# Loading q in 1024-byte rows, four tokens to a partition, with a new order for the first third of a fused retention and token-mixing kernel

## The chip, the cores and the metric

The kernel runs on one core of one Trainium2 chip. The metric is device time in microseconds (us) of one execution. The kernel before has a median of 165.22 us over three runs (165.19 to 165.68).

The engines are named as in the profile: PE is the matrix engine (TensorE) and PEld its weight loads, DVE is VectorE, ACT is ScalarE, POOL is GpSimd, and SP is the sync engine, which only issues transfers. ACT and POOL can issue transfers too, between their other instructions. A row that ends in q, such as SPq or ACTq, is such an issue.

## The reference

There are 4 batches, 8 heads, 768 tokens and a head width of 64, all in float32. Stage one is a recurrent linear attention (RetNet) with a decay per head. Stage two mixes the tokens of its output.

```
state = gamma * state + outer(k_t, v_t)        # per batch and head, t = 0..767
x_t   = q_t @ state / sqrt(64)                 # x: (4, 768, 512), heads side by side
theta = x @ w_theta
y     = w_tok_r @ (x * cos(theta)) + w_tok_i @ (x * sin(theta))     # over tokens
u     = x + y
out   = u + max(u @ w_ch, 0)
```

## The kernel before

**Tiles.** Stage one works in 24 units. Unit n covers one batch, 256 tokens and four heads: a batch has three groups of 256 tokens, and each group has two halves of the heads. For each unit there are three loads of 256 KB (`Lk`, `Lq`, `Lv`, all by `load_unit`, L157). Partition p of a loaded tile holds the tokens 2p and 2p+1 of each of the four heads, so a contiguous row of DRAM is 2 x 64 x 4 = 512 bytes, and a load has 512 such rows.

**Steps of a unit.** The names are those of the order below; the last letter of a token gives the engine or queue (p POOL, v DVE, a ACT, s SP).

- `ck`, `cq` cast k and q to bf16. `cqs` is `cq` with a decay factor (`qsc`) multiplied in, for units whose output is not scaled later by `XA`, and `cv` multiplies v by its factor (`vsc`).
- `Tk`, `Tq` transpose them on PE (L316), and `E` moves the result to SBUF (`kqT`). For some later units a DMA transpose (`Dk`) does both.
- `A` is the score matmul (L346), 16 pieces; `m` multiplies by the causal mask on DVE (L355, 1.2 us).
- `Y` applies the masked scores to v (L423), `I` adds the part from the state (L411), `ST` makes the state's update (L373).
- `S0`, `S1` add up the state, `SB` casts it to bf16 blocks, `XB` or `XA` takes the output out of PSUM into `xT` (`XA` with the decay factor `qx`).

**Steps of stage two**, for each chunk of 128 tokens: `Tx`, `Ex` (or the DMA `Dx`) transpose x; `Hh` is theta (L469, four matmuls 512 wide); `CN` takes sine and cosine on ACT; `z` makes both products; `M.t.s` are the two token-mixing matmuls of output tile t and input chunk s (L509); then `u`, `Tu`/`Eu` or `Du`, `O` (L536), `f`, and the store `SO`. `Tw`, `Ew` transpose the token weights, which `Pw` loads on POOL's own queue, like `Pth` and `Pch` for the other two weights. `Z` is a pair of matmuls on zeros whose result nobody reads.

**The order is written out by hand.** The string `ORDER` lists every step; each engine executes its own steps in that order and waits where data is missing. Nothing is rescheduled. Buffers: 16 for k and q together, 9 for v, 4 for `kqT`, two PSUM banks for transposes, one for scores.

**Transfers.** The framework gives the transfers of SP's and ACT's queues one of eight semaphores in turn, in the order of the string. A transfer is issued only after the transfer eight places before it has landed. So the eight places bound how far loads run ahead, and a queue (or the engine that owns it) stands still until then.

**Start.** `const1` to `const9` and `constA` make the constants: `const2` (POOL memsets and an iota, then a DVE product `arg`), `const3` (ACT: the factors `qsc` and `vsc`), `const8` and `const9` (ACT: eight exponentials for `qx`, L233), `const5` the mask, `const4` the identity, `const6` zeros in the state blocks.

Of the kernel before, what the change touches and what calls it, by code (L numbers as in the profile page):

```python
# [33 lines left out]
SB.5.0.v Tx.3 Tw.1.0 z.1.v SB.5.1.a Ew.1.0.v Ex.3.a CN.2.1 A.6 I.5 Y.5 ST.6 XA.5.0 z.2.v Tw.0.0  # L34
CN.3.0 Tx.4 CN.3.1 Ew.0.0.v S0.6.v XA.5.1 Ex.4.v Hh.4 CN.4.0 CN.4.1 Tw.0.1 M.0.1 Pw.1.1 z.3.v M.0.0
Tw.0.2 Pw.1.2 Ew.0.2.a SB.6.1.a Hh.5 z.4.p SB.6.0.p Lk.9.a M.0.3 ck.7.p cqs.7.p M.0.2 CN.5.1 CN.5.0
cq.8.v m.6 Ew.0.1.v Tw.1.1 Tw.1.2 Ew.1.1.v Lv.9.s M.0.4 M.1.0 Tx.5 Ew.1.2.v M.1.1 S1.6 Tk.7 M.1.4
Pch Ex.5.v z.5.v cv.7.v Tq.8 Tq.7 M.1.2 E.7.a M.0.5 I.6 Y.6 ST.7 A.7 ck.8.a u.0 S0.7.v m.7 XA.6.1
SB.7.1.a M.1.5 M.1.3 XA.6.0 Tw.1.3 M.2.5 Pw.0.2 M.2.3 u.1 S1.7 Tk.8 M.2.1 M.2.0 SB.7.0.v Ew.1.3.a
Tu.0 I.7 cv.8.v E.8.a Lk.10.s ck.10.p cv.9.p Y.7 ST.8 A.8 cqs.9.v ck.9.v M.2.4 Du.1 Eu.0.a XB.7.1.a  # L40
XB.7.0.v S0.8.v SB.8.0.v M.2.2 Tx.6 Tq.9 Tk.9 Lv.10.a cv.10.p Lq.10.s S1.8 u.2 m.8 O.0 E.9.a
SB.8.1.a Hh.6 Tw.1.4 I.8 Y.8 A.9 CN.6.0 Du.2 Lq.14.s CN.6.1 Ex.6.v f.0 ST.9 Tw.0.3 Hh.7 Ew.1.4.v
Ew.0.3.a S0.9.v Tw.0.4 M.3.0 Tw.1.5 CN.7.0 CN.7.1 M.3.2 Dx.7 M.3.1 M.3.5 M.3.3 Lv.12.s Lk.12.s
Ew.1.5.v XA.8.1 Ew.0.4.v Lq.12.s M.3.4 u.3 S1.9 Tw.0.5 Tk.10 M.4.5 cqs.10.p XA.8.0 m.9 M.4.3 Tq.10
SB.9.1.a SB.9.0.a I.9 O.2 Lq.11.s Lk.11.s E.10.a Lk.15.s Ew.0.5.v Lk.14.s Y.9 ST.10 A.10 z.7.p
# [54 lines left out]
def kernel(  # L100
# [13 lines left out]
    nc = tc.nc  # L114
# [532 lines left out]
```

## Time and profile before

| what | value |
|---|---|
| median of the runs | 165.22 us |
| span of the profiled execution, first to last instruction | 163.6 us |
| PE busy | 155.2 us (95%) |
| DVE, ACT, POOL busy | 114.0, 78.9, 74.3 us |
| bytes moved | 34.93 MB, mean 214 GB/s |
| the three kinds of loads | 256 KB each, 5.2 to 6.6 us from issue to landing (median by kind and queue) |
| granted PE clock | 1.000 |

The span leaves out what lies before the first and after the last instruction: 165.22 - 163.6 = 1.6 us against the median of the runs. For the profiled execution itself the span is the only time given. Starts in the answers of the trace are counted from the first instruction. In the page's second part each digit is the busy share of a slice of 4.1 us, and the digits for DMA give the mean over sixteen DMA engines. A row of the windows gives the DMA share as a fraction that can be above 1, since packets of one engine overlap.

### The profile page before, as it was taken

What the parts mean: (1) busy time and instruction counts of PE and PEld (TensorE: products, weight loads), DVE (VectorE), ACT (ScalarE), POOL (GpSimd) and SP (SyncE); (2) the same over time, 40 slices, a digit from 0 to 9 for tenths busy, and PEclk for the clock granted to TensorE, in tenths of its full rate; (3) what the DMA queues carried; (4) which work ended last, traced back from release to release, by engine and by line L of the source; (5) the groups of instructions that cost most, each with busy time, mean ns of one, the idle gap of its engine ahead of it and who ended that gap; (6) DMA issues with size and microseconds to landing.
All of it is one profiled execution on the core that took longest, in us unless ns stands there. A gap on an engine that the chain in (4) does not pass through costs nothing.

```text
span 163.6 us, 4928 instructions
## 1 busy us (share of the span) xinstructions
PE 155.2 (95%) x2034; PEld 87.2 (53%) x2034; DVE 114.0 (70%) x215; ACT 78.9 (48%) x140; POOL 74.3 (45%) x107
## 2 busy tenths in 40 slices
PE   5996889999999999999999999999999999999992
PEld 1453655656666655654554565554545554444561
DVE  3388687887994895984879894887867760345372
ACT  4976697974658255773343726732341616000020
POOL 7557389075034552730227599950469204600000
PEclk9999999999999999999999999999999999999999
DMA  3999999999999999999999999999897548515546
GB/s 115 297 290 255 268 283 236 275 220 286 220 162 232 223 291 139 338 203 270 324 263 198 134 268 221 242 193 298 125 245 136 103 92 227 160 64 128 129 164 224
DMA packets 69062, 34.93 MB, mean 214 GB/s; under 512 B 26416, under 2 KB 66096, under 8 KB 69040
## 3 DMA queue, kind: packets, MB, share of 16 engines
q1 hardware_dynamic: 56032, 23.73, 69.4%
q10 hardware_dynamic: 10320, 7.47, 17.7%
q0 software_dynamic: 2688, 3.41, 12.1%
q8 instruction: 16, 0.26, 0.7%
q14 instruction: 6, 0.05, 0.1%
HBM read 25.69 MB, written 6.29 MB: 196 GB/s over the span
## 4 chain that ended last, share of the span: by engine, by line
PE 76%; DMA 8%; ACT 5%; POOL 3%; issue 2%; SPq 2%; DVE 1%; POOLq 0%; ACTq 0%
PE y_ps L509 36%; PE o_ps L536 11%; PE th_ps L469 10%; DMA kqf<-in_k_dram 8%; PE r_ps L423 3%; ACT qx L233 3%; PE w_ps L491 3%; PE at_ps L346 3%; PE r_ps L411 2%; PE kq_ps L316 2%; SPq L157 2%; PE y_ps L561 2%; ACT cs L476 1%; PE x_ps L455 1%; PE r_ps L373 1%
## 5 line engine op out<-in xcount | busy, mean ns | idle before, releaser
L509 PE MATMUL y_ps<-z,wtr 128*128 128x512 bf16 x138 | 52.4, 380 | 0.0
L509 PE MATMUL y_ps<-z,wti 128*128 128x512 bf16 x138 | 52.3, 379 | 0.0
L483 POOL TENSOR_TENSOR z<-cs,x_sb 128x1024 bf16<-128x1024 bf16 x12 | 25.5, 2136 | 17.9 <-ACT cs L476 10.0
L355 DVE TENSOR_TENSOR at<-at_ps,mask 128x1024 bf16<-128x1024 f32 x24 | 29.2, 1216 | 0.2
L469 PE MATMUL th_ps<-wth,xT 128*128 128x512 bf16 x96 | 24.5, 379 | 0.5 <-ACT cs L476 0.4
L516 DVE TENSOR_TENSOR u<-y_ps,x_sb 128x512 bf16<-128x512 f32 x23 | 15.8, 688 | 12.7 <-PE y_ps L509 12.6
L542 DVE SCALAR_TENSOR_TENSOR ot<-o_ps,u 128x512 f32<-128x512 f32 x22 | 15.1, 688 | 12.5 <-PE o_ps L536 12.4
L308 POOL TENSOR_TENSOR vb<-vf,vsc 128x512 bf16<-128x512 f32 x15 | 15.6, 1041 | 17.3 <-DMA vf<-in_v_dram 16.9
L476 ACT ACTIVATE cs<-th_ps,zerob 128x512 bf16<-128x512 f32 x24 | 16.4, 685 | 13.3 <-PE th_ps L469 8.8
L536 PE MATMUL o_ps<-wch,uT 128*128 128x512 bf16 x88 | 22.6, 379 | 0.0
L476 ACT ACTIVATE cs<-th_ps,halfpi 128x512 bf16<-128x512 f32 x24 | 16.3, 686 | 11.5 <-issue 5.4
L509 PEld LDWEIGHTS <-wtr 128*128 128x128 bf16 x138 | 13.5, 98 | 12.7
L509 PEld LDWEIGHTS <-wti 128*128 128x128 bf16 x138 | 13.5, 98 | 12.0 <-issue 0.2
L139 POOL CAST sbd<-s 64x256 bf16<-64x256 f32 (+1 forms) x21 | 10.1, 481 | 20.8 <-DVE s L391 17.7
L137 ACT COPY kqT<-kq_ps 128x1024 bf16<-128x1024 bf16 x12 | 12.1, 1012 | 11.9 <-PE kq_ps L316 11.9
L469 PEld LDWEIGHTS <-xT 128*128 128x128 bf16 x96 | 8.8, 98 | 8.7 <-issue 0.5
L137 ACT CAST kqb<-kqf 128x512 bf16<-128x512 f32 x16 | 9.6, 620 | 6.9 <-DMA kqf<-in_k_dram 6.3
L536 PEld LDWEIGHTS <-uT 128*128 128x128 bf16 x88 | 8.1, 98 | 8.3
L278 PE MATMUL zz<-zero 128*128 128x512 bf16 x30 | 10.3, 476 | 1.9 <-DVE zero L192 1.9
L423 PE MATMUL r_ps<-at,vb 64*64 64x128 bf16 x384 | 9.9, 221 | 1.6 <-DVE at L355 1.6
L316 PE MATMUL kq_ps<-ident,kqb 128*128 128x128 bf16 x120 | 11.2, 220 | 0.3 <-POOL kqb L302 0.3
L139 POOL CAST kqb<-kqf 128x512 bf16<-128x512 f32 x12 | 7.2, 612 | 8.5 <-DMA kqf<-in_k_dram 8.4
(80 smaller groups left out, 208.7 us busy)
## 6 DMA issues: line engine op xcount, KB each, us to landing
vf<-in_v_dram SPq DMA_DIRECT2D x20, 256.0 KB, 5.9
kqf<-in_k_dram SPq DMA_DIRECT2D x19, 256.0 KB, 5.3
kqf<-in_q_dram SPq DMA_DIRECT2D x17, 256.0 KB, 5.8
out_dram<-ot ACTq DMA_DIRECT2D x12, 256.0 KB, 2.7
out_dram<-ot SPq DMA_DIRECT2D x11, 256.0 KB, 2.9
kqf<-in_q_dram ACTq DMA_DIRECT2D x7, 256.0 KB, 5.2
kqf<-in_k_dram ACTq DMA_DIRECT2D x5, 256.0 KB, 6.6
vf<-in_v_dram ACTq DMA_DIRECT2D x4, 256.0 KB, 5.8
```

Source lines behind the costliest of these rows:

```text
L137: nc.scalar.copy(dst, src)
L139: engines[e].tensor_copy(dst, src)
L308: engines[e].tensor_mul(in_blocks(vb), by_token(raw["vf", n]), _bcast_last(K["vsc"][:, i, :, h * HU:(h + 1) * HU], D))
L355: nc.vector.tensor_mul(at.rearrange("p g j a t -> p (g j) (a t)"), st["at_ps", n].rearrange("p g j a t -> p (g j) (a t)"), _bcast_mid(K["m ...
L423: nc.tensor.matmul(st["R", n + 1][c][g * D:(g + 1) * D, j * P:(j + 1) * P], st["vb", n][rows, lo:lo + D], st["at", n][rows, g, j, a, :], s ...
L469: nc.tensor.matmul(th_ps, st["xT", C][:, j, :], K["wth"][:, j, :], start=(j == 0), stop=(j == 3))
L476: nc.scalar.activation(st["cs", C][:, w, :], st["th_ps", C], AF.Sin, bias=K["zerob" if w else "halfpi"], scale=1.0)
L483: engines[e].tensor_mul(st["z", b][:, c], st["cs", C], _bcast_mid(x_of(C), 2))
L509: nc.tensor.matmul(st["y", t], K["wT"][r][:, s0, t0 * P:(t0 + 1) * P], st["z", b][:, s0, r, :], start=(done == 0 and r == 0), stop=(done = ...
L516: nc.vector.tensor_add(st["u", t], st["y", t], st["x", b][:, t0, :])
L536: nc.tensor.matmul(o_ps, st["uT", t][:, j, :], K["wch"][:, j, :], start=(j == 0), stop=(j == nD - 1))
L542: nc.vector.scalar_tensor_tensor(st["ot", t], st["o", t], 0.0, st["u", t], ALU.max, ALU.add)
```

## The change

Four things are changed.

1. **q's layout and its load.** `Lq` no longer uses `load_unit`. A unit's q is loaded by two transfers of 128 KB, one for each pair of heads. Each fills 64 partitions: partition p of a half holds the four tokens 4p to 4p+3 of two heads, so a row of DRAM is 1024 bytes. The bytes are the same. SP and ACT issue 158 transfers instead of 134, since each of the 24 units now takes two places for q in the round of eight semaphores.
2. **What follows from the layout.** The factor `qsc` gets its own argument `argq`: `const2` has two more iotas and eight more memsets of 64 partitions on POOL, and one more product on DVE. The mask, the casts, the transposed q (`qT`), and the write to `xT` use four-token patterns in place of two-token ones. Sizes of all instructions on PE, DVE, ACT and POOL stay the same: the score and state matmuls read their 128 moving columns in four runs of 32 instead of two of 64.
3. **The order of the first third**, some 420 steps up to `u.3 S1.9 Tw.0.5 Tk.10`, is new on all engines, transfers included. From there on the string is the same as before.
4. Among the steps that change engine in that third: `ck.0` POOL to ACT, `ck.1` ACT to DVE, `ck.2` ACT to POOL, `ck.3` POOL to ACT; `cv.0`, `cv.3` DVE to POOL; `cqs.0`, `cqs.2` DVE to POOL, `cqs.1` POOL to DVE; `E.3`, `E.4` ACT to DVE; `S0.0` DVE to ACT; `XB.1.0`, `XB.1.1`, `XB.3.0`, `XB.3.1` DVE to ACT; `z.3`, `cv.7` and `cqs.9` DVE to POOL; the issues of `Lk.1`, `Lk.3`, `Lv.7`, `Lv.8`, `Lv.9`, `Lq.8`, `Lq.9`, `Lk.10`, `Lq.14` SP to ACT, and that of `Lq.1` ACT to SP.

```
 ORDER, the old first third up to unit 6:
-const2 Lv.0.s const1 const6.v Z.29 Z.2 const5 Z.38 Lk.0.a const3 Z.35 Z.8 Lq.0.s Lv.1.s Z.28 constA
-const4 Lq.1.a const9 Lk.1.s Z.39 const8 ck.0.p Tk.0 ck.1.a cqs.0.v cv.0.v Tq.0 E.0.v Lq.4.a ST.0
-Lk.4.a cqs.1.p Tq.1 Lq.2.s S0.0.v SB.0.1.v A.0 Lk.2.s SB.0.0.p cv.1.p Lv.2.s S1.0 Z.15 I.0 Z.27 m.0
-Tk.1 E.1.a cqs.2.v Z.34 cv.2.p Y.0 ST.1 XB.0.1.a S0.1.v S1.1 SB.1.0.a Pth Lq.3.s Z.18 XB.0.0.v Tq.2
-A.1 SB.1.1.a ck.2.a I.1 m.1 Y.1 ST.2 Tk.2 const7 Z.23 XB.1.0.v Lk.3.s E.2.v XB.1.1.v A.2 ck.3.p
-S0.2.v m.2 S1.2 SB.2.1.a Z.11 cqs.3.p Tq.3 Lv.3.s Tx.0 Tk.3 Z.3 ck.4.p Lv.4.s Lk.5.s Lq.5.s Lv.5.s
-Lq.6.s Lk.6.s Lv.6.s Lq.7.s E.3.a SB.2.0.v I.2 Y.2 XB.2.1.a Ex.0.a cv.3.v cq.4.p Tk.4 Lq.8.s A.3
-ST.3 Lk.7.s S0.3.v SB.3.0.a S1.3 Lv.7.s Lk.8.s Tx.1 Tq.4 SB.3.1.p cv.4.p m.3 Pw.1.0 XB.2.0.a Ex.1.a
-I.3 Lv.8.s E.4.a ck.5.a cq.5.a Y.3 Pw.0.0 ST.4 Hh.0 S0.4.v XB.3.0.v XB.3.1.v cv.5.v CN.0.1 A.4
-CN.0.0 Tq.5 Hh.1 Tk.5 SB.4.0.p SB.4.1.a Pw.0.1 Hh.2 m.4 E.5.v I.4 Y.4 ST.5 ck.6.a Tk.6 Tx.2 cq.6.a
-CN.1.1 CN.1.0 XA.4.1 A.5 XA.4.0 m.5 Lq.9.s Ex.2.v S0.5.v z.0.p Tq.6 E.6.a CN.2.0 cv.6.p Hh.3
 the new one:
+Lv.0.s Lq.0.s const2 Lk.0.a const1 const6.v Z.29 Z.2 const5 Lk.1.a Z.38 const3 constA const4 const9 Z.35
+ck.0.a Z.8 Lq.1.s ck.1.v cv.0.p cqs.0.p Lv.1.s Z.28 Z.39 ST.0 Z.27 Lq.4.a Lq.2.s cqs.1.v Tk.0 cv.1.p Pth
+S0.0.a Tq.0 Tk.1 S1.0 E.0.v Tq.1 Z.23 Lk.3.a Lk.4.a Lk.2.s A.0 Z.11 m.0 SB.0.0.p SB.0.1.a ck.2.p Lv.2.s
+E.1.a const8 I.0 Y.0 ST.1 A.1 cqs.2.p Lq.3.s S0.1.v SB.1.1.p XB.0.0.v m.1 cv.2.p S1.1 Lv.3.s Tq.2 Z.18
+Z.15 Lv.5.s cqs.3.p Z.34 XB.0.1.a SB.1.0.a Tk.2 E.2.v I.1 Y.1 Lv.4.s ck.3.a ST.2 S0.2.v A.2 XB.1.1.a
+Tk.3 XB.1.0.a SB.2.1.p S1.2 Tx.1 cv.3.p Tq.3 m.2 SB.2.0.a Z.3 cq.4.p ck.4.p Ex.1.a I.2 Y.2 E.3.v Lk.5.s
+ST.3 A.3 S0.3.v const7 Tx.0 Hh.0 SB.3.0.a cv.4.p m.3 Ex.0.a Lq.5.s SB.3.1.v Lv.6.s XB.2.0.a XB.2.1.a
+Lq.6.s Hh.1 S1.3 CN.0.1 cv.5.v Pw.1.0 Tk.4 CN.1.1 Pw.0.0 Tq.4 E.4.v CN.1.0 I.3 Lk.6.s Y.3 ST.4 S0.4.v
+XB.3.0.a Pw.0.1 A.4 cq.5.v SB.4.1.a SB.4.0.p Lq.7.s XB.3.1.a Tq.5 ck.5.a Hh.2 Tk.5 m.4 Pw.1.1 Tx.2 I.4
+CN.0.0 cv.6.p Y.4 z.1.v E.5.v ST.5 A.5 cq.6.a S0.5.v ck.6.a Tk.6 Ex.2.v XA.4.1 Lk.7.s Tq.6 Hh.3 CN.2.1
+XA.4.0 SB.5.1.p SB.5.0.a z.0.p m.5 E.6.a Tw.1.0 I.5 CN.2.0 Tx.3 Ew.1.0.v Y.5 ST.6 Ex.3.a A.6 CN.3.0
...
     def Lq(n, e):
-        load_unit("qf", q, n, e)
+        b, i, h = unit(n)
+        t = io.tile([P, 2, 4, D], FT, name="kqf", bufs=16)
+        for j in range(2):
+            h0 = h * HU + 2 * j
+            queues[e].dma_start(
+                out=t[j * D:(j + 1) * D].rearrange("p g a d -> p g (a d)"),
+                in_=q[b, h0:h0 + 2, i * 2 * P:(i + 1) * 2 * P, :].rearrange(
+                    "g (p a) d -> p g (a d)", a=4))
+        raw["qf", n] = t
...
+        posq = const.tile([P, nI, 4], FT, name="posq")
+        lgq = const.tile([P, H // 2], FT, name="lgq")
+        for j in range(2):
+            rows = slice(j * D, (j + 1) * D)
+            nc.gpsimd.iota(posq[rows], pattern=[[2 * P, nI], [1, 4]], base=1,
+                           channel_multiplier=4, allow_small_or_imprecise_dtypes=True)
+            for x in range(H // 2):
+                head = x // 2 * HU + 2 * j + x % 2
+                nc.gpsimd.memset(lgq[rows, x:x + 1], math.log(gammas[head]))
...
+        argq = const.tile([P, nI * 4, H // 2], FT, name="argq")
+        nc.vector.tensor_mul(argq, _bcast_last(posq.rearrange("p i a -> p (i a)"), H // 2),
+                             _bcast_mid(lgq, nI * 4))
+        K["argq"] = argq
...
+    def qT(n, rows, j, c):
+        lo = j * D + c * (D // 2)
+        return st["kqT", n][rows, 1, :, lo:lo + D // 2]
...
                         nc.tensor.matmul(at_ps[cols, g, j, a, :],
-                                         kqT[rows, 0, a, j, cols],
-                                         kqT[rows, 1, :, j, cols],
+                                         kqT[rows, 0, 2 * a + j, cols],
+                                         qT(n, rows, j, c),
...
                 nc.tensor.matmul(r[c][:, j * P:(j + 1) * P], sbd_of(n)[:, c, j, :],
-                                 st["kqT", n][:, 1, :, j, c * D:(c + 1) * D],
+                                 qT(n, slice(0, P), j, c),
...
-        return (st["xT", C][:, 2 * h:2 * h + 2].rearrange("p j (t a) -> p j t a", a=2),
-                st["R", n + 1][c][:, :2 * P].rearrange("p (j a t) -> p j t a", j=2, a=2))
+        return (st["xT", C][:, 2 * h:2 * h + 2].rearrange("p j (t a) -> p j t a", a=4),
+                st["R", n + 1][c][:, :2 * P].rearrange("p (j a t) -> p j t a", j=2, a=4))
```

More of the change, by code (lines that the diff above doesn't have):

```diff
@@ new lines @@
+XB.10.1.a CN.8.0 SB.11.1.p cv.12.p Lq.16.s I.11 Tk.14 Ex.8.v A.12 Y.11 ST.12 f.4 Lv.15.s O.3 z.8.p
+E.14.a XA.11.0 XA.11.1 Hh.10 S0.12.a f.3 SB.12.0.v Tx.10 Tu.5 CN.10.1 Dx.11 Ex.10.v cq.13.p Lk.16.s
+Lv.17.s Hh.11 SO.2.s CN.10.0 m.12 S1.12 z.10.v Tk.15 M.6.1 M.6.2 M.6.0 M.6.3 CN.11.0 CN.11.1 M.7.3
+SB.12.1.a Lk.17.a ck.13.a M.7.4 M.7.0 M.6.4 Dk.13 M.7.1 z.11.v M.6.5 SO.3.s A.14 M.7.2 Eu.5.v I.12
+Lv.14.s u.6 cqs.15.v M.7.5 M.9.3 Tq.15 ck.17.a E.15.a m.14 SO.4.a Lq.17.s Lq.18.s Lk.21.s ck.16.a M.9.0
@@ L236, in const3 @@
     def const3():
-        K["qsc"] = const.tile([P, nI, 2, H], FT, name="qsc")
+        K["qsc"] = const.tile([P, nI, 4, H // 2], FT, name="qsc")
         K["vsc"] = const.tile([P, nI, 2, H], FT, name="vsc")
-        for t, bias, sc in ((K["qsc"], K["lscale"], 1.0), (K["vsc"], K["zerob"], -1.0)):
-            nc.scalar.activation(t.rearrange("p i a h -> p (i a) h"), K["arg"], AF.Exp,
+        for t, arg, bias, sc in ((K["qsc"], K["argq"], K["lscale"], 1.0),
+                                 (K["vsc"], K["arg"], K["zerob"], -1.0)):
+            nc.scalar.activation(t.rearrange("p i a h -> p (i a) h"), arg, AF.Exp,
                                  bias=bias, scale=sc)
@@ L259, in const5 @@
     def const5():
-        mask = const.tile([P, 2, 2, D], BF, name="mask")
+        mask = const.tile([P, 2, 4, D // 2], BF, name="mask")
         nc.gpsimd.memset(mask, 1.0)
```

113 lines of the change are left out of this document (53 added, 60 removed).

## The prediction

> **What bounds the kernel now.** I read the page's slices first, then PE's waits, then the chain that ended last, and then the places in time of the score matmuls.
>
> ```profile
> span 163.6 us, 4928 instructions
> ...
> PE   5996889999999999999999999999999999999992
> ...
> DMA  3999999999999999999999999999897548515546
> ```
>
> PE is full from the eighth slice (28.6 us) to the last. Only the first seven slices have room, and there the transfers are full too. The kernel ends earlier only if PE's dense stretch begins earlier or starts with more of its work done. PE's longest wait of all is at the start:
>
> ```profile
> PE zz L278 <- DVE zero L192: 1.9, 1, 1.9
> ```
>
> The chain shows what fills the room later on:
>
> ```profile
> 9.32 6.61 DMA kqf<-in_k_dram
> 15.94 0.37 SPq L157
> ...
> 19.31 5.96 DMA kqf<-in_k_dram
> 25.37 1.14 ACT kqb L137 x2
> ...
> 37.11 0.22 PE x_ps L455 x4
> 37.33 0.43 PE y_ps L509 x2
> ```
>
> k of unit 4 is issued at 9.32 and lands at 15.93. SP issues the next load at 15.94, at once: it is the transfer eight places on, and it had waited for that landing. k of unit 6 lands at 25.27 and ACT casts it at 25.37. So up to 25 us the landings set the pace, and their issues hang on earlier landings. The last two rows are prices: four transposes 0.22, two matmuls 512 wide 0.43. `Hh` is thus 0.86 and a `Z` 0.43.
>
> The windows of the score matmuls of units 0 to 6 are my milestones (start:end, then busy times, granted clock, DMA share, GB/s):
>
> ```profile
> 8.80:9.15 0.35, 0.35 (x16) 0.25 (x16) 1.00 1.21 291
> 12.12:12.47 0.35, 0.35 (x16) 0.25 (x16) 1.00 1.25 293
> 15.56:15.91 0.35, 0.35 (x16) 0.25 (x16) 1.00 1.04 173
> 18.78:19.03 0.25, 0.25 (x16) 0.25 (x16) 1.00 1.13 330
> 22.71:23.07 0.36, 0.35 (x16) 0.26 (x16) 1.00 1.21 292
> 26.59:26.94 0.35, 0.35 (x16) 0.26 (x16) 1.00 1.17 217
> 29.27:29.64 0.37, 0.37 (x16) 0.26 (x16) 1.00 1.07 292
> ```
>
> Up to A.5 a unit takes 3.2 to 3.9 us. At A.2 the transfers run at only 173 GB/s: that is the eight places holding issues back.
>
> **q's transfers.** The nearest rows are a stretch in which only 512-byte rows move, and the end, where stores of 2 KB and 1 KB rows move (last two columns: share, GB/s):
>
> ```profile
> 3.00:9.00 6.00, 5.73 (x55) 2.62 (x54) 2.27 (x5) 5.57 (x11) 3.62 (x14) 1.00 1.20 303
> 160.50:162.30 1.80, 0.07 (x1) 0.00 (x0) 0.10 (x1) 0.00 (x0) 0.00 (x0) 1.00 0.88 315
> ```
>
> A load of 262 KB takes 0.87 us at 303 GB/s. Per unit of share the stream gives 253 GB/s with 512-byte rows and 358 with the long ones, so a q of 1024-byte rows costs between 0.61 us (as the stores) and 0.87 (nothing gained). Two issues where there was one could make it dearer still, so the upper end is 0.95. I take 0.65, near the stores, because the end mixes 1 KB with 2 KB. That is 0.2 us a unit, 1.5 us by unit 6 and 5 us over 24 units, all of it off PE's path unless a landing is what PE waits for.
>
> [...]
>
> **The start.**
>
> ```profile
> 1.02 0.32 POOL L209 MEMSET lg<- 128x1 f32 x8
> ...
> 3.68 1.07 POOL L228 MEMSET lgp<- 64x1 f32 x8
> ```
> ```profile
> 3.95 4.90 ACT L233 ACTIVATE qx<-pos,lscale,lgp 128x512 f32<-128x512 f32 x8 [0.43 <-POOL lgp L228]
> 8.85 0.62 ACT L137 CAST kqb<-kqf 128x512 bf16<-128x512 f32 x1
> ```
> ```profile
> 1.92 5.58 PE L278 MATMUL zz<-zero 128*128 128x512 bf16 x14 [1.92 <-DVE zero L192]
> 7.34 0.61 PE L316 MATMUL kq_ps<-ident,kqb 128*128 128x128 bf16 x8
> ```
>
> Eight memsets take 0.32 us on 128 partitions and 1.07 on 64. The new ones are of the second form: I take 1.07 with 0.2 for two iotas, so 1.3, and 0.5 as the low end. `arg`, a second product of 0.2, the zeros and with them PE's first `Z` come at 3.4 instead of 1.92. The same seven `Z` stand first and last 5.42, so PE is free at 8.85. ACT meets the longer constants too: `lgp` and with it `const9`, the four wide ones of the eight exponentials (some 2.85 us of the 4.90), start at 5.25 and end at 8.1. `ck.0`, now behind them, is done at 8.7. That is just covered by the `Z`; without that cover each us there would cost one.
>
> Then PE goes `ST.0`, a `Z`, four groups of transposes and a `Z` (0.2 + 0.43 + 0.89 + 0.43): A.0 at 10.8, two us late. Unit 1 is already transposed by then. `m` decides the next steps:
>
> ```profile
> L355 DVE TENSOR_TENSOR at<-at_ps,mask 128x1024 bf16<-128x1024 f32 x24 | 29.2, 1216 | 0.2
> ...
> L308 POOL TENSOR_TENSOR vb<-vf,vsc 128x512 bf16<-128x512 f32 x15 | 15.6, 1041 | 17.3 <-DMA vf<-in_v_dram 16.9
> ...
> L137 ACT COPY kqT<-kq_ps 128x1024 bf16<-128x1024 bf16 x12 | 12.1, 1012 | 11.9 <-PE kq_ps L316 11.9
> ...
> L139 DVE COPY kqT<-kq_ps 128x1024 bf16<-128x1024 bf16 x3 | 2.1, 684 | 0.5 <-PE kq_ps L316 0.5
> ```
>
> A.0 ends 11.15, `m.0` 12.5, `Y.0` and `ST.1` take 0.45: A.1 at 13.0 against 12.12. `m.1` ends 15.05, and meanwhile PE spends three `Z` (1.3); `Y.1`, `ST.2` and `E.2` on DVE give A.2 at 16.0 against 15.56, with one `Z` more behind it: level.
>
> **Units 3 to 6.** ACT issues q of unit 4 behind `const9`, at 8.1. q of unit 3 stands eight places after it, so it is issued when that lands (two of the small transfers, 11 to 12), behind k3, k4 and the 512 KB of `w_theta`, and lands near 16.5, v3 a us later. POOL's `cqs.3` and `cv.3` (1.04 each, the same form of instruction; POOL has taken four of these from DVE and given back `cqs.1`, `ck.0` and `ck.3`) end near 19: ST.3 at 19.0, A.3 at 19.2 against 18.78. This is the latest point of the new order.
>
> From there it gains. A.3 ends at 19.45; `Tx.0` (0.22), `Hh.0` and `Hh.1` (1.72, now both ahead of A.4, in time that was spent waiting), `Tk.4` and `Tq.4` (0.44), `I.3`, `Y.3` and `ST.4` (0.65) lead to 22.5. `E.4` is on DVE (0.68, on ACT it was 1.01) and ends at 22.7: A.4 at 22.75 against 22.71, with one `Hh`, 0.86 of work, more behind it.
>
> The next landings: up to q5 there are twelve loads of k and v (10.4), six q's (3.9) and `w_theta` (1.8); from 3 us on that is 19.1, and 2 us go to held-back issues: q5 at 21.2, k6 three loads later at 23.7. That is 1.5 us before the 25.27 above, the seven q's saving.
>
> After A.4, ACT is the tight engine: it has given up `E.3` and `E.4` (1.0 each) and taken four `XB`, `ck.0` and `ck.3`. `Hh.2` waits for `XB.3.0` behind three sines and cosines (23.4 to 24.3), `Tk.5` for `ck.5` (24.65 to 24.9), four short steps of 0.85 follow: A.5 at 25.8 against 26.59, with `Tk.6` (0.22) less done. `ck.6` ends at 26.3; `Tk.6`, `Tq.6`, `Hh.3`, a transpose of weights (0.33), then `I.5`, `Tx.3`, `Y.5` and `ST.6` (0.9) lead to 28.9: A.6 there against 29.27, with `I.5`, `Y.5` and `ST.6` (0.7) already done. That is 1.05 ahead. I take 0.25 off for `Tq.8`, which waits for `cq.8` behind `m.6` on DVE.
>
> Edits at nothing: the four 32-wide runs and four-token patterns (same instruction sizes; `A` is 0.35 a unit and `I` some 0.22, 13 us in all, so 2% slower reads would cost 0.25), the moved `z.3` (POOL is 1.5 us ahead of M.0.3), the eight issues on ACT at 30 to 40 us (0.4 each, in a stretch where ACT waits for PE).
>
> **After the first third** the order is the same, and PE carries 0.8 us through if loads keep up. Split q's make the eight places shallower: 24 more transfers in the same round. The tightest place I find is v of unit 11:
>
> ```profile
> 63.57 1.04 POOL L308 TENSOR_TENSOR vb<-vf,vsc 128x512 bf16<-128x512 f32 x1 [4.00 <-DMA vf<-in_v_dram]
> ```
> ```profile
> 65.11 0.29 PE L373 MATMUL r_ps<-vb,kqb 64*64 64x64 bf16 x16
> ```
>
> POOL starts at its landing and ends 0.5 us before PE's `ST.11`. With PE 0.8 earlier, v11 must land 0.3 earlier. Six halves of q ahead of it are shorter, but its issue hangs on a landing eight smaller places back: 0 to 1.0 us, and I take 0.
>
> **Sum.** 163.6 - 0.8 = 162.8 for the span; with the 1.6 us outside it, 164.4 against the median of 165.22. A difference under 0.3% (0.5 us) is about what a measurement of this kernel cannot tell from none.
>
> **Rivals.**
> - Start and landings push the other way, slower, 166.4: q3 hangs on q4's landing and v3 on q3's. If v3 lands 2 us later than my 17.5, ST.3 and all behind it move to 21, the 0.8 turns into -1.2. It decides from a landing of v3 at 18.3. For it: A.3 is late in my own walk, and the chain above shows issue waiting for landing. Against: the `Hh` are there to fill.
> - The split stalls an engine later, slower, 166.2: where the transfer eight places back is late, ACT stands with its casts and sines behind its own issue of q (`Lq.19`, `Lq.22`) and PE, which has no room there, loses about 1 us net. Against: ACT has idle time at most of these places.
> - Gained, then given back at v11 or its like, 165.1.
> [...]
>
> **Chances.** Forecast 0.46; start slower 0.20; stall later 0.11; given back 0.13; no gain by rows 0.10. Faster by over 0.3% is the forecast alone, 0.46. Within 0.3% are the given-back case and half of the rows case: 0.18. Slower: 0.36. The low end is 163.0: the short memsets (0.8 us less), q's at 0.61 (0.3 by unit 6) and no wait at `Tq.8` (0.25). The high end, 166.8, is the first rival with its landing 0.4 us later still. The forecast's own range is 163.0 to 164.7.
>
> **What would show it.** PE's first `Z` near 3.4, A.0 near 10.8, A.3 near 19.2, A.6 before 29.3 with `ST.6` ahead of it; ACT casting `ck.0` at 8.1; a landing of k6 before 24.5; PE full from 29 us. Wrong if A.6 is later than 29.9, or if PE shows a wait of over 0.5 us behind 30 us, above all at `ST.11`.

## The result, and the profile after

The changed kernel takes 175.06 us (median of four runs, 172.33 to 175.89). The kernel before, run beside it, takes 165.3. The ratio is 1.048, with a 95% interval of 1.040 to 1.056: slower. The forecast was 164.4, in a range up to 166.8. The ratio is made from the two shorter runs of the changed kernel (172.33 and 174.69 us), so it stands for some 8 us where the medians differ by 9.8, and the profiled execution took 175.43 us, so its trace shows some 2 us more than the ratio does.

The page after, with the same slices as before, and its two lines on q's issues:

```profile
span 173.7 us, 4940 instructions
...
PE   3987497985999999999999999889999999999993
...
PEclk9999969997899999999999999999999999999999
DMA  4999999959995999999999999999868837516446
...
kqf<-in_q_dram SPq DMA_DIRECT2D x30, 128.0 KB, 4.8
...
kqf<-in_q_dram ACTq DMA_DIRECT2D x18, 128.0 KB, 4.0
```

PE is busy 156.2 us, 1 us more than before, so most of the 10 us are waiting. PE has most of its gaps up to slice ten (43 us), and two dips of the granted clock, which was 1.000 throughout before. The transfers have gaps of their own. The windows of the first 48 us (start:end, length, then busy times, granted clock, DMA share, GB/s), of the kernel before:

```profile
0.00:8.50 8.50, 6.31 (x39) 2.66 (x40) 3.37 (x9) 6.39 (x11) 5.66 (x34) 1.00 0.82 209
8.50:12.00 3.50, 3.50 (x70) 2.13 (x70) 3.00 (x8) 2.41 (x5) 1.71 (x3) 1.00 1.22 290
12.00:18.00 6.00, 4.32 (x96) 2.72 (x93) 5.29 (x11) 3.78 (x7) 4.33 (x6) 1.00 1.21 239
18.00:24.00 6.00, 5.04 (x128) 3.42 (x125) 4.05 (x9) 5.36 (x11) 3.57 (x6) 1.00 1.19 302
```

and of the changed kernel:

```profile
0.00:8.50 8.50, 5.70 (x30) 2.05 (x31) 2.41 (x9) 5.28 (x8) 6.92 (x44) 1.00 0.82 200
8.50:12.00 3.50, 2.96 (x49) 1.78 (x41) 2.50 (x4) 2.50 (x5) 2.22 (x3) 1.00 1.18 254
12.00:18.00 6.00, 4.18 (x119) 2.89 (x119) 4.17 (x9) 3.69 (x10) 2.96 (x4) 1.00 1.21 254
18.00:24.00 6.00, 3.89 (x64) 2.58 (x67) 2.83 (x6) 3.21 (x7) 5.30 (x8) 0.75 1.19 275
24.00:30.00 6.00, 5.35 (x116) 3.42 (x115) 4.99 (x8) 5.05 (x10) 3.34 (x5) 0.96 1.17 235
...
36.00:42.00 6.00, 3.58 (x32) 2.15 (x31) 4.91 (x8) 2.75 (x4) 5.43 (x5) 0.96 0.73 185
42.00:48.00 6.00, 5.95 (x78) 3.69 (x77) 4.97 (x7) 1.01 (x1) 2.50 (x3) 0.76 1.08 171
```

Multiply GB/s by length and add: by 24 us the kernel before had moved 6.04 MB, the changed one 5.76 MB at nearly the same shares. It is short by one load of k or v. The clock was at half in two stretches of 3.4 us:

```profile
21.00:24.40 3.40, 3.00 (x44) 1.78 (x41) 2.30 (x5) 1.56 (x5) 3.40 (x7) 0.50 1.18 230
41.50:44.90 3.40, 3.40 (x23) 2.57 (x24) 2.53 (x4) 0.86 (x1) 3.00 (x3) 0.50 1.04 150
```

PE was busy for 3.00 and 3.40 us of them. Of its matmuls 512 wide, those at 42.09 and 42.52 start 0.43 us apart, those at 45.33 and 45.54, at the full clock, 0.21. So an estimate of the clock's part is half of the busy time, 3.2 us.

The chain that ended last, in the changed kernel, from the first transfer on:

```profile
1.32 5.16 DMA kqf<-in_q_dram
6.48 0.02 issue
6.50 4.19 DMA kqf<-in_q_dram
10.69 0.02 issue
10.71 7.71 DMA kqf<-in_q_dram
...
18.56 1.05 POOL kqb L324
```

Each of these transfers of q is issued the moment the one eight places before it lands. The third is the second half of unit 3's q; it lands at 18.42, and POOL scales it at once. The score matmuls of units 0, 3, 4 and 6 (start, duration), where the kernel before had 8.80, 18.78, 22.71 and 29.27:

```profile
10.36 0.42 PE L372 MATMUL at_ps<-kqT 64*64 64x128 bf16 x16
...
21.43 0.66 PE L372 MATMUL at_ps<-kqT 64*64 64x128 bf16 x16
26.54 0.42 PE L372 MATMUL at_ps<-kqT 64*64 64x128 bf16 x16
...
33.26 0.40 PE L372 MATMUL at_ps<-kqT 64*64 64x128 bf16 x16
```

### The profile page after: what moved, and what is told of

Same layout as the page of the kernel before. It is cut to its first block, busy times and chain, and to the rows that moved or that the text cites. A ratio compares the mean times of both kernels' runs of the same rounds, so it can differ in the third digit from the quotient of the medians.

```text
span 173.7 us, 4940 instructions
## 1 busy us (share of the span) xinstructions
PE 156.2 (90%) x2005; PEld 88.6 (51%) x2034; DVE 117.4 (68%) x210; ACT 77.9 (45%) x142; POOL 81.5 (47%) x121
## 4 chain that ended last, share of the span: by engine, by line
PE 55%; DMA 24%; DVE 10%; issue 4%; POOL 3%; SPq 1%; ACT 1%; ACTq 0%; POOLq 0%; DVEq 0%
PE y_ps L535 24%; DMA kqf<-in_q_dram 13%; PE o_ps L562 8%; PE th_ps L495 8%; DMA x_sb<-xT 7%; DMA vf<-in_v_dram 4%; PE r_ps L449 3%; DVE sbd L137 2%; PE at_ps L372 2%; DVE at L381 2%; PE kq_ps L338 2%; PE y_ps L587 2%; PE r_ps L437 2%; PE r_ps L399 2%; DVE z L509 1%
## 5 line engine op out<-in xcount | busy, mean ns | idle before, releaser
L535 PE MATMUL y_ps<-z,wtr 128*128 128x512 bf16 x133 | 50.9, 383 | 0.4
L535 PE MATMUL y_ps<-z,wti 128*128 128x512 bf16 x130 | 49.5, 381 | 0.7 <-issue 0.6
L509 POOL TENSOR_TENSOR z<-cs,x_sb 128x1024 bf16<-128x1024 bf16 x13 | 27.8, 2144 | 14.4 <-ACT cs L502 9.8
L381 DVE TENSOR_TENSOR at<-at_ps,mask 128x1024 bf16<-128x1024 f32 x24 | 29.2, 1216 | 0.8 <-PE at_ps L372 0.6
L330 POOL TENSOR_TENSOR vb<-vf,vsc 128x512 bf16<-128x512 f32 x17 | 17.9, 1055 | 24.6 <-DMA vf<-in_v_dram 24.2
L568 DVE SCALAR_TENSOR_TENSOR ot<-o_ps,u 128x512 f32<-128x512 f32 x22 | 15.1, 688 | 13.5 <-PE o_ps L562 13.4
L542 DVE TENSOR_TENSOR u<-y_ps,x_sb 128x512 bf16<-128x512 f32 x23 | 15.8, 688 | 11.5 <-PE y_ps L535 11.4
L502 ACT ACTIVATE cs<-th_ps,zerob 128x512 bf16<-128x512 f32 x24 | 16.5, 686 | 15.2 <-PE th_ps L495 10.4
L137 POOL CAST sbd<-s 64x256 bf16<-64x256 f32 (+1 forms) x22 | 10.7, 485 | 20.6 <-DVE s L417 16.6
L535 PEld LDWEIGHTS <-wti 128*128 128x128 bf16 x138 | 13.6, 98 | 12.5 <-issue 0.2
L135 ACT COPY kqT<-kq_ps 128x1024 bf16<-128x1024 bf16 x10 | 10.1, 1011 | 8.0 <-PE kq_ps L338 7.8
L338 PEld LDWEIGHTS <-kqb 128*128 128x128 bf16 x120 | 8.3, 101 | 7.9 <-POOL kqb L324 3.4
L300 PE MATMUL zz<-zero 128*128 128x512 bf16 x27 | 9.3, 480 | 2.9 <-DVE zero L200 2.8
L135 ACT CAST kqb<-kqf 128x512 bf16<-128x512 f32 x14 | 8.4, 616 | 7.3 <-DMA kqf<-in_k_dram 5.7
L324 POOL TENSOR_TENSOR kqb<-kqf,qsc 128x512 bf16<-128x512 f32 x9 | 9.6, 1075 | 3.3 <-DMA kqf<-in_q_dram 3.3
```

What stands on the lines that cost most here:

```text
L135: nc.scalar.copy(dst, src)
L137: engines[e].tensor_copy(dst, src)
L330: engines[e].tensor_mul(in_blocks(vb), by_token(raw["vf", n]), _bcast_last(K["vsc"][:, i, :, h * HU:(h + 1) * HU], D))
L338: nc.tensor.transpose(st["kq_ps", n][:, 4 * w + x, :], st["kqb", n][:, w, x * P:(x + 1) * P], K["ident"])
L381: nc.vector.tensor_mul(at.rearrange("p g j a t -> p (g j) (a t)"), st["at_ps", n].rearrange("p g j a t -> p (g j) (a t)"), _bcast_mid(K["m ...
L502: nc.scalar.activation(st["cs", C][:, w, :], st["th_ps", C], AF.Sin, bias=K["zerob" if w else "halfpi"], scale=1.0)
```

## The experiments

Two theories stood at the start. O: the new order loses the time, in three places that the trace shows. T: the two transfers of q lose it. All times below are medians; the kernel before had 165.4 to 165.8 us in the same sessions. Starts of `A.n` are the first rows of the score matmuls in each trace. A trace is of one execution: that of the mended order took 167.87 us, 1.5 above its median, and the others of the table lie within 0.8 of theirs. Between the old order and the new, A.10 and A.19 have the same work in front of them; the earlier starts do not.

| kernel | us | ratio (95%) | A.3 | A.6 | A.7 | A.10 | A.19 |
|---|---|---|---|---|---|---|---|
| before | 165.4 | 1 | 18.8 | 29.3 | 40.1 | 57.0 | 106.9 |
| changed | 175.06 | 1.048 (1.040-1.056) | 21.4 | 33.3 | 47.4 | 65.3 | 117.0 |
| old order, new layout | 175.70 | 1.058 (1.052-1.065) | 27.7 | 38.3 | 49.5 | 66.4 | 117.7 |
| old order, two by heads | 171.17 | 1.033 (1.029-1.038) | 21.2 | 34.8 | 45.6 | 62.5 | 112.4 |
| old order, two by partitions | 176.37 | 1.064 (1.062-1.067) | 23.6 | 36.3 | 47.3 | 64.5 | 117.2 |
| the same, from q6 on only | 171.18 | 1.032 (1.027-1.036) | 18.7 | 29.3 | 40.1 | 58.4 | 112.5 |
| new order, old layout, one transfer | 167.94 | 1.013 (1.010-1.016) | 18.2 | 29.2 | 41.2 | 59.6 | 109.4 |
| new order, two by heads | 168.46 | 1.018 (1.014-1.021) | 18.8 | 29.5 | 41.5 | 59.6 | 109.6 |
| new order, two by partitions | 174.92 | 1.056 (1.051-1.061) | 22.0 | 32.5 | 44.9 | 63.1 | 115.8 |
| new order, two by parity | 173.21 | 1.048 (1.040-1.055) | 20.8 | 31.2 | 43.7 | 62.1 | 114.6 |
| new order mended, one transfer | 166.38 | 1.005 (1.002-1.008) | 18.3 | 29.6 | 41.6 | 59.3 | 109.2 |

### Each part alone

The layout alone: the changed code with the old string.

```
-ORDER = new first third
+ORDER = the string of the kernel before
```

> The changed code (q in 1024-byte rows, two DMAs a unit, the new constants) with the kernel before's order. Theory O (the new order of the first third loses the time; the layout by itself costs little): 165.5 to 167.5 us, because the only costs are the longer run of constants at the start (about 0.7 us to ck.0 and the first Z in the trace of after) and q landings some 0.25 us later each, for which the old order left room from the fourth unit on. Theory T (the transfer itself loses it: 1.1 us a unit of q where it was 0.87, a second issue and a second semaphore place each): 171 us or more, with the fourth to seventh units each late by what their q is late.

175.70 us: theory T. The windows of the layout alone:

```profile
12.00:18.00 6.00, 4.45 (x114) 2.46 (x112) 4.82 (x11) 4.43 (x8) 1.92 (x2) 1.00 0.77 145
18.00:24.00 6.00, 0.05 (x1) 0.06 (x2) 1.99 (x4) 0.00 (x0) 1.72 (x3) 0.78 1.16 251
```

From 12 to 18 us the DMA engines run at a share of 0.77 instead of 1.21; for the next six PE does nothing.

The order alone: the kernel before with the new string.

```
-ORDER = the string of the kernel before
+ORDER = new first third
```

> The new order with the code before (q in 512-byte rows, one DMA a unit). Theory O: 171 us or more, with the same stalls in the same places (VectorE's casts of s held beside POOL's z at 34 to 40 us, SP silent behind Du.2 until about 50 us). Theory T: 167 us or less, since every q lands sooner and the chain behind the fourth unit's q closes up.

167.94 us, where the kernel before had 165.76 in the same session. So the order loses 2.2 us by itself, and theory O is wrong about the size. The two parts do not add up (9.9 + 2.2 against 9.8): the new order is made for the layout and absorbs some of its loss.

### What of the two transfers is dear

Three kernels with the old order: q in two transfers without any other change, by heads (all 128 partitions) or by partition halves, both with 512-byte rows; and the layout with some halves issued by POOL, whose transfers are not in the round of eight.

```
     for j in range(2):                                  # by heads
+        dma(out=t[:, 2*j:2*j+2], in_=q[heads 2j, 2j+1])
     for j in range(2):                                  # by partitions
+        dma(out=t[j*64:(j+1)*64], in_=q[tokens of these partitions])
```

> The kernel before with nothing changed but q's load: two DMAs a unit, each of all 128 partitions and two heads, 512-byte rows. Theory N (the number of transfers loses the time: each transfer waits for the one eight places before it, so twice the transfers of q means that fewer bytes are under way and that q3's and k4's issues hang on landings): 171 to 177 us, near the 175.7 of the layout alone, with the DMA share between 8.5 and 18 us near 0.75 instead of 1.21. Theory H (a transfer that writes 64 partitions is slower): 165 to 167.5 us. Theory R (the 1024-byte rows, or the copies and masks of the new layout): 165 to 167.5 us.

> The kernel before with q in two DMAs a unit, each of 64 partitions and four heads, 512-byte rows. Theory N: as by heads within 1.5 us, 171 to 177 us. Theory H: 171 us or more, and over 3 us above the load by heads. Theory R: 165 to 167.5 us.

```
-            queues[e].dma_start(
+            (nc.gpsimd if j and 2 <= n < 8 else queues[e]).dma_start(
```

> The layout alone (the order of before), with the second half of q2 to q7 issued by POOL, whose transfers have semaphores of their own: the SP and ACT round then carries as many transfers in that stretch as before. Theory N: 166.5 to 170.5 us instead of 175.7, DMA share of 8.5 to 18 us back over 1.0, no idle 6 us of TensorE at 18 to 24; it keeps some loss for POOL's six issues (0.6 to 0.9 us each). Theory H and theory R: 173 us or more, since the halves and the rows are the same.

By heads 171.17, by partitions 176.37: neither theory alone. In the old order the number of transfers is worth 5.8 us, the 64 partitions another 5.2, and the rows of 1024 bytes with their longer constants give back 0.7 in medians (175.70), which the intervals do not separate. By heads, a window of the two transfers:

```profile
12.00:18.00 6.00, 3.69 (x99) 2.07 (x87) 4.93 (x10) 3.72 (x8) 2.64 (x4) 1.00 0.88 178
```

A share of 0.88 where one transfer had 1.21 fits the eight places holding issues back, as theory N says.

The kernel with halves on POOL took 175.61 us. That is what theories H and R expected (173 or more) and not N's 166.5 to 170.5, although the share came back, as N expected (1.19 and 1.21 in the two windows below).

```profile
8.50:12.00 3.50, 2.86 (x52) 1.62 (x50) 2.63 (x5) 1.97 (x5) 2.93 (x4) 1.00 1.19 249
12.00:18.00 6.00, 2.58 (x89) 1.70 (x88) 2.68 (x5) 3.32 (x6) 3.15 (x4) 0.98 1.21 232
```

Its trace says why this tells little against N: POOL, busy with its casts, issued the second half of unit 3's q only at 14.49, behind `w_theta` at 13.70 on the same queue. It landed at 21.4, and POOL waited 5.64 us for it. One wait was exchanged for another.

### The same under the new order

Here the number of transfers and their partitions come apart.

```
 ORDER = new first third, code before
+Lq: two transfers by heads / by partitions
```

> The new order and the code before, with q in two DMAs of 128 partitions and two heads each. It stands to the order alone (167.9 us) as only the number of transfers differs. Theory N (the number; the new order does not absorb it): 172 us or more. Theory H (64 partitions): at most 169.5 us, since these halves move at the same 291 GB/s as whole units.

> The new order and the code before, with q in two DMAs of 64 partitions and 512-byte rows (222 GB/s where whole units showed 290). Theory H: 173 to 178 us, and at or above the changed kernel's 175.1, whose 1024-byte rows moved at about 260 GB/s. Theory N: as by heads, within 1.5 us.

168.46 and 174.92 us, both as theory H expects. So in medians: the order +2.2 against the kernel before; two transfers instead of one +0.5 against the order alone, with intervals that overlap; 64 partitions instead of 128 in each +6.5; rows of 1024 bytes and the constants for them +0.1, where the runs of the changed kernel alone spread over 3.6. The new order does what a round of eight places needs; what it cannot absorb is the 64 partitions.

The rate of q's transfers is read from windows in which q's packets fill the stream. In this trace a landing shows about a microsecond after the packets have moved: between the landings of q's halves at 7.01 and 8.15 us in the changed kernel, 548 packets carry 0.29 MB, some 530 bytes each, so most of them belong to another load. The windows below therefore lie ahead of the landings. (The 222 and 260 GB/s of the expectations come from windows between landings.) By heads, 512-byte rows:

```profile
5.25:7.06 1.81, 1.46 (x10) 0.69 (x8) 0.33 (x1) 1.81 (x4) 0.69 (x2) 1.00 1.22 291
```

By partitions with the new order, 512-byte rows:

```profile
8.50:10.00 1.50, 1.47 (x19) 1.07 (x18) 1.43 (x3) 0.64 (x3) 0.69 (x1) 1.00 1.23 248
```

In the changed kernel, 1024-byte rows, with the packets of the same window:

```profile
8.50:10.00 1.50, 1.50 (x29) 1.20 (x20) 1.12 (x3) 0.56 (x2) 0.88 (x1) 1.00 1.16 242
DMA packets 398, 0.36 MB, mean 242 GB/s; under 512 B 42, under 2 KB 398, under 8 KB 398
```

Two more kernels put the even partitions into one transfer and the odd ones into the other. With 512-byte rows:

```profile
6.42:7.78 1.36, 1.36 (x20) 0.48 (x18) 0.27 (x1) 0.98 (x2) 0.75 (x1) 1.00 1.22 291
```

and with 1024-byte rows:

```profile
5.50:6.50 1.00, 1.00 (x5) 0.33 (x4) 0.44 (x1) 1.00 (x3) 0.93 (x3) 1.00 1.09 343
```

So a transfer to one half of the partitions is slower, 242 to 248 GB/s against 291, and in halves the longer rows gain nothing. Spread over even and odd partitions they moved at 343. Whether the rows did that is not shown: in the kernel by parity with 512-byte rows the stream reaches 334 GB/s between 10.5 and 12.0 us. By partitions and by parity a transfer has 64 of them, so with 512-byte rows it is their place in one half that goes with 248 GB/s instead of 291; why a half is slower, no run shows.

The load by even and odd partitions, with 512-byte rows:

```
-                out=t[j * D:(j + 1) * D], in_=q[tokens of these partitions]
+                out=t[j::2],              in_=q[tokens of the even / odd partitions]
```

> The new order and the code before, with q in two DMAs of 64 partitions each, as in the load by partitions (174.9 us), but one takes the even and one the odd partitions; rows of 512 bytes. If a transfer is slow because its 64 partitions lie in one half of the memory (theory P, place): 168 to 169.5 us, as the load by heads (168.5), with its transfers near 290 GB/s. If it is slow because it has only 64 partitions, or because its issue takes 0.60 us instead of 0.37 to 0.50 (theory C, count): 173.5 to 176 us. [...]

173.21 us: at full rate, and still 4.7 us over the load by heads. So the rate is worth 1.7 us of the 6.5 in medians, with intervals that overlap. What else the halves keep is a longer issue. Instructions of the line of `Lq` (count: shortest/median/longest in ns), by heads:

```profile
L168 ACTq DMA_DIRECT2D kqf<-in_q_dram x18: 374/481/531, 5.1 to 104.9; - x18
```

by parity:

```profile
L168 ACTq DMA_DIRECT2D kqf<-in_q_dram x18: 608/624/1235, 5.1 to 110.0; - x18
```

and in the changed kernel:

```profile
L171 ACTq DMA_DIRECT2D kqf<-in_q_dram x18: 602/618/799, 5.6 to 112.3; - x18
```

An issue of 64 partitions takes 0.60 us or more whatever the rows, where one of 128 partitions and the same bytes takes 0.37 at the least. By the medians of SP (0.62 against 0.47, 30 issues) and ACT (0.62 against 0.48, 18 issues) that is 7 us of the two queues. That this is the remaining 4.7 us is argued, not shown: no run changed the issue time alone.

The starts say where the 4.7 us arise. By parity A.2 comes at 18.4 instead of 15.8, and A.10 to A.19 takes 52.5 us instead of 50.0. Ahead of A.2 the stream runs short, here by heads and then by parity:

```profile
9.00:10.50 1.50, 1.35 (x29) 0.84 (x27) 0.76 (x2) 1.22 (x2) 1.50 (x2) 1.00 1.17 285
9.00:10.50 1.50, 1.35 (x25) 0.62 (x23) 0.88 (x2) 1.40 (x3) 1.50 (x2) 1.00 0.87 209
```

POOL casts k of unit 2 at 12.59 instead of 11.46, PE waits 2.0 us for unit 2 instead of 0.6, and behind that the granted clock is 0.50 from 13.9 to 17.3 us with PE busy for 2.83, an estimate of 1.4 us. By heads it is 1.00 throughout.

### Where along the kernel

```
     def Lq(n, e):
+        if n < 6: one transfer, as before
+        else: two by partitions
```

> The kernel before with q0 to q5 whole and q6 to q23 in two DMAs of 64 partitions (176.4 us when all units are so). If the loss arises only while the loads run just ahead of TensorE, in the first 30 us: 165.4 to 167.5 us. If every divided unit adds to it: 172 us or more (18 of 24 units, so three quarters of 11 us).

171.18 us, near the second figure (172 or more) and far from the first. Up to A.7 this kernel is the one before to 0.1 us; then it loses 1.4 by A.10 and 5.6 by A.19. Waits of PE from 42 to 115 us, a stretch in which the kernel before has none:

```profile
PE r_ps L420 <- issue: 1.4, 1, 1.4
...
PE r_ps L382 <- POOL vb L317: 0.8, 1, 0.8
...
PE o_ps L545 <- DMA wch<-in_moe_w_ch_dram: 0.7, 1, 0.7
PE o_ps L545 <- DMA uT<-u: 0.5, 1, 0.5
```

So the q's divided late cost too. The table's last two columns say the same: from A.10 to A.19 the kernel before takes 49.9 us, the two kernels by heads 49.9 and 50.0, and those of the table with 64 partitions 51.2 to 54.0.

### The order's own places

The trace of the changed kernel holds VectorE beside POOL. VectorE's rows there:

```profile
35.48 1.55 DVE L137 CAST sbd<-s 64x128 bf16<-64x128 f32 x1
...
38.26 1.70 DVE L137 CAST sbd<-s 64x128 bf16<-64x128 f32 x1
```

and POOL's:

```profile
34.83 2.13 POOL L509 TENSOR_TENSOR z<-cs,x_sb 128x1024 bf16<-128x1024 bf16 x1 [0.59 <-ACT cs L502]
37.51 2.37 POOL L509 TENSOR_TENSOR z<-cs,x_sb 128x1024 bf16<-128x1024 bf16 x1 [0.55 <-DVE x_sb L137]
```

The casts end when POOL's products end (37.0 and 39.9). On POOL the same cast takes 0.30, and on VectorE in the kernel before 0.28. Both casts are new on VectorE: the old order has `SB.6.0` on POOL and `SB.6.1` on ACT. The product beside the first is `z.3`, which the new order moves to POOL; the one beside the second is `z.4`, which POOL made before too. PE then waits for what is behind them:

```profile
40.60 0.38 PE L481 MATMUL x_ps<-ident,xT 128*128 128x128 bf16 x4 [1.71 <-DVE wtr L137]
```

What holds the casts is not shown; the rows show that they end with POOL's products. Not everything beside a product is held: VectorE's `xT` at 37.82, beside the second, takes 0.41, and the one at 33.49, beside no `z`, 0.42.

```
-... SB.6.0.v ... SB.6.1.v ...
+... SB.6.0.a ... SB.6.1.a ...
```

> The changed kernel with SB.6.0 and SB.6.1 on ScalarE instead of VectorE. If VectorE's two casts of 1.55 and 1.70 us (0.28 elsewhere) are the loss of 35 to 41 us, and they are the only instructions that POOL's z holds: 171.5 to 173.5 us against the changed kernel's 172.3 to 175.9, the wait of PE's x_ps behind VectorE at 40.6 gone. If POOL's z holds whatever VectorE runs next (z.5, Ew.0.2, Ew.0.1), the hold only moves to these and the time stays within 0.5 us of the changed kernel. Theory T expects no gain either.

174.62 us, ratio 1.043 (1.039 to 1.048): no gain that the intervals separate. In its trace the wait of `x_ps` is gone and A.7 comes 4.2 us sooner than in the changed kernel, A.10 4.5, but A.19 only 2.7. One hold moved to another cast (`kqb`, 1.33 us); the rest was lost again behind A.10, where the loads are late.

```
-... Du.2 ... Lq.10.s ... Lk.12.s ...
+... Lq.10.s Lk.12.s Du.2 ...
```

> The changed kernel with q10 and k12 issued on SP ahead of Du.2 instead of behind it. If SP's silence from 28 to 53 us is a loss of its own (DMA share 0.73 to 0.82 there, all later loads some 10 us late): 1 to 2.5 us less than the changed kernel, the small PE waits behind 85 us smaller. If the loads behind it had slack enough: within 0.5 us of the changed kernel.

175.45 us: no gain. SP's silence has slack behind it in this kernel; other waits came (1.6 us for `uT` near 113 us).

Both mends on the order alone, with one transfer of q:

> The order alone (167.9 us) with SB.6.0 and SB.6.1 on ScalarE and q10 and k12 ahead of Du.2 on SP. If the order's own loss is VectorE held beside POOL's z (x_ps waits 1.7 us) and SP's silence: 165.0 to 166.5 us, so level with the kernel before. If other places of the order lose it: within 0.5 us of 167.9.

166.38 us, 1.6 under the order alone. There the mends are kept; that the loads keep up there is the likely reason, which no run separates. It remains 0.5% above the kernel before; what the order still loses, no run shows.

### w_theta, and all mends together

```
-cv.1.p Pth ... SB.1.1.p
+cv.1.p ... SB.1.1.p Pth             # far back
-cv.1.p Pth ... ck.2.p
+cv.1.p ... ck.2.p Pth               # between
```

> The changed kernel with w_theta's load on POOL moved from behind cv.1 to behind SB.1.1 (about 10.1 to 14.1 us). Theory W (the second half of q3, issued at 10.71 because of the eight places and the 0.60 us issues, and v3 behind it share the DMA engines with w_theta's 512 KB, so that q3 lands at 18.4 and v3 at 19.7 instead of about 15): q3 by 15.5 us, A.3 at 18.8 to 19.8 us instead of 21.3, and 172 to 174 us, or 170 to 172.5 where the granted clock stays at 1.0. If w_theta is only exchanged for another late load (Hh.0 waits for it): within 1 us of the changed kernel's 175.1.

> The changed kernel with w_theta's load behind ck.2 on POOL, so issued near 12.7 us: after q3's second half (10.7) and v3 (11.4), yet 1.4 us before the place that made Hh.0 wait 4.6 us. If the loss is only that one meeting: q3 by 15.5, w_theta by 20.5, A.3 near 19.3, A.4 near 24 instead of 26.2, and 172 to 174 us. If the bytes of the first 25 us are what is short (every place only exchanges one late load for another): A.4 at 26 us or later and 174.5 to 177.5 us.

176.99 and 176.59 us: moving it loses. With the load far back A.3 came at 19.1 instead of 21.4, as expected; the next product then waited for `w_theta`:

```profile
PE th_ps L495 <- DMA wth<-in_moe_w_theta_dram: 4.6, 1, 4.6
```

and between the two places:

```profile
PE th_ps L495 <- DMA wth<-in_moe_w_theta_dram: 2.8, 1, 2.8
```

`A.4` was at 29.9 and 28.5 instead of 26.5. So each of the two places exchanges one late load for another, as expected if the bytes of the first 25 us are what is short.

> The load by even and odd partitions (512-byte rows, new order, 173.2 us) with w_theta behind ck.2. Its halves move at the rate of whole units, so if its 4.7 us over the load by heads come from the 0.60 us issues putting q3's second half (issued 10.0, landed 17.9) behind w_theta (issued 9.7): 168.5 to 170.5 us. If they come from elsewhere: 172 us or more.

171.94 us with the full-rate halves: 1.3 of their 4.7 us, between the two expectations. This one is not settled.

> The changed kernel with all three mends of its order: w_theta later, SB.6.0 and SB.6.1 on ScalarE, q10 and k12 ahead of Du.2. If these places are where the dearer transfers turn into waits, they add up: 167.5 to 170.5 us. If the transfers of 64 partitions limit the first 60 us by themselves, the loads are late anyway and it stays at 171.5 us or more. Below the kernel before (165.4 us) neither theory expects it.

175.85 us: the mends do not add up. One of them, `w_theta` far back, loses by itself; otherwise this is what was expected if 64-partition transfers make the loads late anyway.

### The change repaired

The changed kernel with even and odd partitions, then also with the mended order.

```
-                out=t[j * D:(j + 1) * D]
+                out=t[j::2]
-        lo = j * D + c * (D // 2)
-        return kqT[rows, 1, :, lo:lo + D // 2]
+        return kqT[rows, 1, :, c * D + j:(c + 1) * D:2]
+        # const2: a parity column for posq and lgq
```

> The changed kernel (1024-byte rows, new order) with each unit's two DMAs on the even and on the odd partitions; the constants of q are built from a parity column (some nine small instructions on POOL and VectorE at the start, about 1 us) and the products read q's columns with a step of two. Theory P: 166.5 to 169.5 us, so at least 5 us under the changed kernel's 175.1; below the load by heads (168.5) only if 1024-byte rows are worth more than the constants. Theory C: 173.5 us or more.

> The same with the mended order (SB.6.0 and SB.6.1 on ScalarE, q10 and k12 ahead of Du.2), which took 1.6 us off the order alone. Theory P: 165 to 168 us. Theory C: 172 us or more.

The first ran from 172.2 to 181.4 us (median 180.93), too far apart for a ratio; the second from 169.7 to 180.3 (median 175.33), and its two shortest runs give a ratio of 1.030 (1.022 to 1.038). Both miss the figures that theory P gave, and their medians lie where theory C put them. By its two shortest runs the second is the best kernel with 1024-byte rows, and still slower than the kernel before. No version beat the kernel before.

Their traces speak against the long issue as the cost of the late q's. From A.10 to A.19 they take 50.5 and 50.3 us, close to the 49.9 of the kernel before, with issues of q as long as in the load by parity with 512-byte rows, which takes 52.5. These two traces are of executions of 172.2 and 171.5 us, below the medians, so this is a hint and not a proof. A single transfer with 1024-byte rows over all 128 partitions was not tried: in this layout the partitions follow two strides of DRAM.

## Why the prediction was wrong

**q's transfers, 0.65 us a unit.** This step failed. The halves of q land 0.56 to 0.58 us apart, so a unit costs 1.1 us, more than my upper end of 0.95. I took the shares of whole 128-partition transfers (253 and 358 GB/s per unit of share) and let only the row length vary. In halves the row length made no difference (242 GB/s against 248 with 512-byte rows, 175.06 us against 174.92); that each transfer fills only one half of the partitions made one (248 GB/s against 291, 174.92 us against 168.46). No row of before shows a transfer to half of the partitions, and the 0.95 allowed for a second issue only. Even 1.1 us is not the whole price: with the rate back at 291, 4.7 of the 6.5 us remain, and what they are stays open. The case of no gain by rows, to which I gave 0.10, falls short too: it leaves a q at its old price, 0.87 us, where the two halves took 1.1.

**The start.** Roughly right. The memsets took 0.4 and not 1.07 (my low end was 0.5), the first `Z` came at 2.77 instead of 3.4, A.0 at 10.36 instead of 10.8, A.1 at 12.5 instead of 13.0.

**Units 3 to 6.** q3 landed at 18.42 instead of 16.5, v3 at 19.74 instead of 17.5, A.3 came at 21.4 instead of 19.2 and A.6 at 33.3 instead of 28.9. The second half of q3 was issued at 10.71, behind `w_theta` at 10.11, and took 7.7 us to land; by heads it was issued at 9.72, just ahead of `w_theta` at 9.73, and POOL scaled it at 15.1. The first rival named this place and its threshold, a landing of v3 at 18.3, and gave it 0.20. Its mechanism was the right one, for the changed kernel's first 21 us. Its price, 2.0 us less work ahead, held for A.3 (2.2 late against my own walk) and not beyond.

**"Edits at nothing".** Two of these were wrong. `z.3` on POOL was covered by the time of M.0.3, as I wrote; I did not ask what runs on VectorE beside it and beside `z.4`. There the new order has put `SB.6.0` and `SB.6.1`, a move that I did not price, and their casts were held for 2.7 us in all. It is part of the 1.6 us that the mends won back in the order alone. And I priced the extra issues of ACT at 0.4 each; those of q take 0.60.

**The clock.** It had no term at all, since before it was 1.000 everywhere. In the trace above it was 0.50 for 3.4 us twice, behind waits of PE (2.2 us up to 19.66, 1.7 us up to 40.60), an estimate of 3.2 us. Not every wait did that: the new order by heads has a wait of 1.7 us for `x_ps` too, and a clock of 1.00 throughout. A forecast of a wait of 2 us at PE has to allow for it.

**"After the first third PE carries 0.8 us through if loads keep up."** They do not. I looked for one tight place (v11) and took 0 for it. The row of DMA slices that I quoted stands at nine from slice 2 to slice 28 (115 us), and I read it only for the first seven. A dearer transfer can be paid wherever the DMA engines are full, which is two thirds of this kernel: with q0 to q5 whole, the rest still costs 5.6 us by A.19. Nor does the order by itself carry a lead: with one transfer for q it is level at A.6 and 2.5 us behind at A.10 (59.6 against 57.0), lost in steps that I did not walk.

**What held.** In the order with one transfer A.3 is 0.6 us ahead and A.6 0.1 (my walk, for two, had 0.4 behind and 0.4 ahead), with `Hh` pulled forward; the round of eight places is what the new order is built around, and it absorbs some 5 of the 5.8 us that two transfers cost in the old one.

## What to carry to other kernels

Divide a load by its free dimension (heads), not by partitions: two transfers of 128 partitions cost 0.5 us here under an order made for them, two of 64 cost 7.0. Where the DMA share is near its highest for most of the span (1.21 from 30 to 60 us and 1.20 from 60 to 115 in the kernel before), price a change of a transfer over all transfers of that stretch, and expect a mend of one wait to come back as another. A rate read for a row length in one shape of transfer says little of another shape: here 358 GB/s per unit of share in the stores, and 209 (242 over 1.16) in the halves of q. Set the window for a rate by the packets and not by the landings.

## What the runs showed that I had not expected

- 128 KB to one half of the partitions moved at 242 to 248 GB/s with rows of either length, and at 291 with 512-byte rows when spread over even or odd partitions.
- An issue of 64 partitions takes 0.60 to 0.63 us in any layout (shortest and median), one of 128 partitions with the same bytes 0.37 to 0.48.
- The granted clock fell after some waits and stayed low: 0.51 in a stretch of six microseconds behind the 4.6 us wait for `w_theta`:

```profile
24.00:30.00 6.00, 5.27 (x59) 3.06 (x63) 0.69 (x1) 1.95 (x3) 0.00 (x0) 0.51 1.16 230
```
